# Weight tiles loaded by two transfers, and the transfers of two queues pinned to one order

## The chip, the core and the metric

The kernel runs on one core of a Trainium2 chip. The time is device microseconds (us) of that core, from the start of the program to its end; a run is one execution. The profile is one more execution, taken by the hardware profiler: its span goes from the first to the last instruction, and every start in the text is counted from the span's start.

The core's engines work beside each other, each through its own list of instructions in order: TensorE (PE; PEld is its weight load), VectorE (DVE), ScalarE (ACT), GpSimd (POOL) and SyncE (SP), which only starts transfers. Transfers between memory and on-chip memory are started by SyncE and ScalarE here (a few at the start by GpSimd) and carried out by 16 DMA engines that all of them share. "SPq" and "ACTq" stand for an engine's sequencer, which issues transfers.

## The reference

Two blocks, one after the other. The first is a delta rule over 768 tokens for 4 batches of 8 heads, with head size 48; the second takes its output as 3072 tokens of 384 features.

```python
def _attn_ref(q, k, v, beta) -> np.ndarray:
    B, H, S, D = q.shape
    k_n = k / (np.linalg.norm(k, axis=-1, keepdims=True) + 1e-06)
    state = np.zeros((B, H, D, D), dtype=np.float32)
    y = np.zeros_like(q)
    for t in range(S):
        kt, vt, bt = (k_n[:, :, t], v[:, :, t], beta[:, :, t, None])
        y[:, :, t] = np.einsum('bhd,bhde->bhe', q[:, :, t], state)
        v_old = np.einsum('bhde,bhd->bhe', state, kt)
        state = state + bt[:, :, :, None] * np.einsum('bhd,bhe->bhde', kt, vt - v_old)
    return y.astype(np.float32)
...
def _moe_ref(x, w_in, w_out) -> np.ndarray:
    h = x @ w_in
    g = h * np.cos(h)
    return (g @ w_out).astype(np.float32)
```

w_in is 384 x 2048 and w_out 2048 x 384, both in 64-bit floats; q, k, v and beta are 32-bit.

## The kernel before

**Tokens.** The 768 tokens of a batch are cut into 24 units of 32. For a unit the kernel loads q, k and v (`load`, line 341, and from unit 8 on, for the transposed q and k, `load_blocks`, line 369), forms the products of its keys and queries (`gram`), solves a triangular system for its 32 steps, brings the state forward (`update`) and makes the unit's outputs (`within`). The triangular matrices of two units are inverted together, twelve times in all, by GpSimd (`invert`, line 702; the first by VectorE). Their way goes through memory, since the rows have to be laid out anew: `gram_put` (line 652) writes g to g_dr, `gram_get` (line 667) reads it back as gb, the inverse z is written by `put` (line 739) to z_dr, and `get` (line 746) reads it back as zt, or for the first two units as halves_z. The factors of the solve in TensorE are zt and the right side.

**Features.** Every two units make 256 tokens (4 batches of 32 each) of the second block, twelve steps in all: the product with w_in (`hidden`, line 930, in the first two steps, and `layer`, line 1109, with sums of blocks after them), h cos(h) (lines 974 to 1000) and the product with w_out (`output` and `product`, lines 1134 and 1189), whose result is stored by `store`.

**Weights.** The weights come in 28 tiles, listed in `narrows` (line 455): 12 of w_in, 128 rows by 512 values, and 16 of w_out, 128 rows by 384 values. A value is two 32-bit words, so a row of a tile is 1024 or 768 words, 4096 or 3072 bytes, and a tile 512 or 384 KB. `narrow_load` (line 469) loads a tile into a buffer called pairs by one transfer. `narrow_split`, `narrow_shift` and `narrow_add` then make 32-bit floats of it, on ScalarE, VectorE and GpSimd; each of them works on the whole tile. The buffers are of the tag "g", of which there are eight, shared with the blocks of g.

**Order.** The program is a list of tasks, and `Order.LINE` (line 83) is a sequence of their numbers, written out by hand, in which the tasks are emitted. `Order.OTHER` (line 50) is the set of tasks that take the other engine of two: `queue` (line 335) gives a transfer to ScalarE where its task is in that set, and to SyncE otherwise. `pin` (line 1697) adds a dependency that the compiler's scheduler keeps and that makes no wait on the chip. The last lines of the kernel pin every instruction to the one before it of the same engine, so each engine runs its own instructions in the written order. How the instructions of different engines stand among each other in the compiled program is settled by the compiler's scheduler, apart from the buffers' first users, which `wrote` (line 1709) pins across engines.

**Semaphores of transfers.** There are 526 transfers of SyncE and 139 of ScalarE, 665 in all. They share eight completion semaphores, given out in turn in the order in which the scheduler has laid the transfers of both queues. A transfer waits in its engine's sequencer until the transfer that had its semaphore before, the eighth before it in that order, has landed. Behind a waiting transfer of ScalarE stand ScalarE's own computations.

Of the kernel before, what the change touches and what calls it, by code (L numbers as in the profile page):

```python
# [218 lines left out]
def kernel(  # L219
# [115 lines left out]
    def queue(*key):  # L335
        return nc.scalar if key in Order.OTHER else nc.sync
# [60 lines left out]
    for b in range(B):  # L397
        nc.gpsimd.dma_start(
            out=bq[C * b : C * b + H].rearrange("p n t -> p (n t)"), in_=beta[b]
# [67 lines left out]
    words = {}  # L467

    def narrow_load(t):
        _, src, n = narrows[t]  # L470
        pairs = ffn_pool.tile([128, 4, TOK], U32, name="pairs", tag="g", bufs=GATES)
        words[t] = pairs.rearrange("p a t -> p (a t)")[:, 0 : 2 * n]
        queue("weights", t).dma_start(out=words[t], in_=src)
        words[t] = words[t].rearrange("p (n two) -> p n two", two=2)

    def narrow_split(t):
# [777 lines left out]
    def store(p, i, cols=slice(0, DM)):  # L1254
# [12 lines left out]
            x=2, x_sum=XS, turns=2, g=GATES, o=2, o_out=2,  # L1267
# [396 lines left out]
    def weights(t):  # L1664
        c = 1.0 if t < 12 else 0.78
        add(("weights", t), "SP", 0.45, lambda: narrow_load(t),
            [("weights", t - 1)] if t else [],
            makes=[("g", ("pairs", t))], moves=1.8 * c, due=LOADS + 2 * t)
        add(("split", t), "ACT", 1.4 * c, lambda: narrow_split(t), [("weights", t)])
        add(("shift", t), "DVE", 1.4 * c, lambda: narrow_shift(t), [("split", t)])  # L1670
        add(("add", t), "POOL", 1.45 * c, lambda: narrow_add(t), [("shift", t)],
            uses=[("pairs", t)], due=W_IN + 2 * t if t < 12 else W_OUT + 2 * (t - 12))
# [24 lines left out]
    def pin(ins, on):  # L1697
        tc.add_manual_dep(
            ins,
            on.name,  # L1700
            mybir.DependencyInfo(
                mybir.DependencyClass.NoSync, mybir.DependencyReason.DATA
            ),
            reason="order",
        )
# [12 lines left out]
    order.run(wrote)  # L1718


    last = {}
    for ins in nc.cur_bb.bb.instructions:
        if ins.engine in last:
            pin(ins, last[ins.engine])
        last[ins.engine] = ins


# [29 lines left out]
```

## Time and profile before

| | us |
|---|---|
| three runs | 667.28, 664.82, 667.79 |
| median | 667.28 |
| the profiled execution's span | 663.5 |
| TensorE busy | 595.1 (90%) |
| TensorE's weight load busy | 559.0 (84%) |
| VectorE busy | 504.2 (76%) |
| GpSimd busy | 484.3 (73%) |
| ScalarE busy | 294.7 (44%) |

TensorE's busy time by stretch, with its granted clock and the share of time that the DMA engines are busy:

| stretch, us | TensorE busy, us | clock | DMA share |
|---|---|---|---|
| 0 to 25 | 10.85 | 1.00 | 0.82 |
| 25 to 50 | 3.32 | 0.59 | 0.81 |
| 50 to 76 | 15.14 | 0.50 | 0.71 |
| 76 to 150 | 67.04 | 0.94 | 0.63 |
| 150 to 240 | 88.38 | 1.00 | 0.39 |

Transfers issued, from the page's last part (name, queue, count, size):

```profile
pairs<-in_moe_w_out_dram SPq DMA_DIRECT2D x12, 384.0 KB
vp<-in_v_dram SPq DMA_DIRECT2D x88, 48.0 KB
pairs<-in_moe_w_in_dram ACTq DMA_DIRECT2D x7, 512.0 KB
gb<-g_dr ACTq DMA_DIRECT2D x12, 256.0 KB
kp<-in_k_dram SPq DMA_DIRECT2D x128, 24.0 KB
...
pairs<-in_moe_w_in_dram SPq DMA_DIRECT2D x5, 512.0 KB
```

In rows of the profile "out<-in" names what an instruction writes and reads, "L473" is line 473 of the kernel, and an arrow in brackets tells what ended the idle time before an instruction. A "chain" is the work that ended last, followed back from the end: each link is what released the next one.

### The profile page before, as it was taken

The numbers are of one execution on the slowest core, as the hardware profiler recorded it, in microseconds if no ns is written. First come the engines' busy times: TensorE is split into PE (matmuls) and PEld (weight loads), VectorE is DVE, ScalarE is ACT, GpSimd is POOL, SyncE is SP. The second block draws the span as 40 slices with busy tenths as digits, with TensorE's granted clock in tenths as the row PEclk, the third lists the DMA queues.
The fourth block names the chain that finished last, engine by engine and source line by source line (L and its number), as shares of the span: only waits on it lengthen the run. The fifth ranks groups of instructions, "written<-read, shape, count | busy, mean of one in ns | idle before, by whom it ended". The sixth has DMA issues, their size and how long they took to land.

```text
span 663.5 us, 23460 instructions
## 1 busy us (share of the span) xinstructions
PE 595.1 (90%) x9784; PEld 559.0 (84%) x9784; DVE 504.2 (76%) x996; ACT 294.7 (44%) x518; POOL 484.3 (73%) x852
## 2 busy tenths in 40 slices
PE   3315799889999999999999999999789999999997
PEld 3304698677898999989999999999789999999996
DVE  5775588689799887868888888898758678667581
ACT  3424475454234544545545436444235453546340
POOL 4447888868898898888898988988666688413322
PEclk9855599989999999999999999999989999999999
DMA  8786764762164352344451462542311400200000
GB/s 173 166 185 155 180 139 120 156 133 43 44 113 62 64 94 43 74 85 71 67 100 27 80 98 41 95 78 52 73 24 33 92 10 26 34 2 26 1 24 25
DMA packets 215629, 51.52 MB, mean 78 GB/s; under 512 B 207076, under 2 KB 210420, under 8 KB 215524
## 3 DMA queue, kind: packets, MB, share of 16 engines
q1 hardware_dynamic: 160372, 32.31, 26.4%
q10 hardware_dynamic: 54896, 17.28, 12.1%
q8 instruction: 77, 1.26, 0.8%
q0 software_dynamic: 256, 0.45, 0.3%
q14 instruction: 28, 0.23, 0.1%
HBM read 39.24 MB, written 10.75 MB: 75 GB/s over the span
## 4 chain that ended last, share of the span: by engine, by line
PE 61%; POOL 19%; DMA 7%; DVE 4%; issue 4%; SPq 2%; ACT 1%; ACTq 0%; POOLq 0%; DVEq 0%
PE p_h L1113 20%; PE p_out L1193 20%; POOL z L728 8%; POOL part L721 7%; PE p_h L935 6%; PE p_out L1136 3%; DMA vp<-in_v_dram 3%; PE p_kq L781 2%; POOL x_sum L1028 2%; PE p_s L876 2%; PE p_kq L893 2%; PE p_u L851 2%; PE p_o L1193 2%; DMA pairs<-in_moe_w_in_dram 1%; PE p_g L611 1%
## 5 line engine op out<-in xcount | busy, mean ns | idle before, releaser
L721 POOL TENSOR_TENSOR part<-z,gb 128x126 f32<-128x126 f32 (+22 forms) x341 | 151.9, 445 | 36.2 <-ACT z L700 8.2
L728 POOL TENSOR_TENSOR z<-z,part 128x126 f32<-128x126 f32 (+22 forms) x341 | 155.3, 455 | 26.7
L1193 PE MATMUL p_out<-w_out,g_ffn 128*128 128x192 f32 x672 | 120.0, 329 | 0.0
L1193 PEld LDWEIGHTS p_out<-w_out,g_ffn 128*128 128x128 f32 x672 | 108.0, 190 | 1.2
L1209 POOL TENSOR_TENSOR g_ffn<-g_ffn 128x512 f32<-128x512 f32 x43 | 57.8, 1349 | 56.6 <-PE p_out L1193 30.9
L1113 PE MATMUL p_h<-x_sum,w_in 128*128 128x128 f32 x640 | 83.2, 279 | 7.9 <-ACT g_ffn L1125 6.4
L1193 PE MATMUL p_out<-w_sum,g_ffn 128*128 128x192 f32 x496 | 88.9, 328 | 0.1
L992 ACT ACTIVATE turns<-turns,halfpi 128x512 f32<-128x512 f32 x96 | 68.3, 719 | 42.5 <-DVE turns L983 35.6
L1113 PEld LDWEIGHTS p_h<-x_sum,w_in 128*128 128x128 f32 x640 | 78.4, 193 | 9.2 <-ACT g_ffn L1125 6.7
L1193 PEld LDWEIGHTS p_out<-w_sum,g_ffn 128*128 128x128 f32 x496 | 79.6, 190 | 0.7 <-DVE o L1245 0.3
L976 ACT ACTIVATE turns<-g_ffn,quarter_turn 128x512 int32<-128x512 f32 x70 | 50.1, 720 | 48.8 <-DVE g_ffn L1130 25.7
L1130 DVE TENSOR_TENSOR g_ffn<-g_ffn,p_h 128x512 f32<-128x512 f32 x80 | 54.6, 683 | 17.0 <-PE p_h L1113 14.9
L906 ACT COPY y<-p_kq 32x384 f32<-32x384 f32 x96 | 45.1, 470 | 37.2 <-PE p_kq L893 31.9
L995 DVE TENSOR_TENSOR g_ffn<-turns,g_ffn 128x512 f32<-128x512 f32 x70 | 53.3, 770 | 8.9 <-ACT turns L992 8.8
L983 DVE SCALAR_TENSOR_TENSOR turns<-g_ffn,turns 128x512 f32<-128x512 f32 x70 | 56.5, 812 | 1.6 <-ACT turns L976 1.4
L1113 PE MATMUL p_h<-x_sum,in_sum 128*128 128x128 f32 x400 | 53.8, 279 | 0.1
L935 PE MATMUL p_h<-x_ffn,w_in 128*128 128x128 f32 x384 | 48.8, 288 | 5.5 <-DVE g_ffn L995 5.5
L935 PEld LDWEIGHTS p_h<-x_ffn,w_in 128*128 128x128 f32 x384 | 46.9, 202 | 6.6 <-DVE g_ffn L995 5.9
L1113 PEld LDWEIGHTS p_h<-x_sum,in_sum 128*128 128x128 f32 x400 | 50.0, 194 | 0.9 <-ACT g_ffn L1125 0.4
L1245 DVE SCALAR_TENSOR_TENSOR o<-p_out,o 128x192 f32<-128x192 f32 x74 | 25.2, 353 | 31.5 <-PE p_out L1193 30.6
L530 POOL TENSOR_TENSOR knrm<-ksum,halves 128x16 f32<-128x16 f32 (+1 forms) x14 | 38.9, 2777 | 11.1 <-DVE ksum L518 11.0
L1113 PE MATMUL p_h<-x_ffn,w_in 128*128 128x128 f32 x320 | 43.1, 279 | 0.0
(133 smaller groups left out, 1011.0 us busy)
## 6 DMA issues: line engine op xcount, KB each, us to landing
pairs<-in_moe_w_out_dram SPq DMA_DIRECT2D x12, 384.0 KB
vp<-in_v_dram SPq DMA_DIRECT2D x88, 48.0 KB
pairs<-in_moe_w_in_dram ACTq DMA_DIRECT2D x7, 512.0 KB
gb<-g_dr ACTq DMA_DIRECT2D x12, 256.0 KB
kp<-in_k_dram SPq DMA_DIRECT2D x128, 24.0 KB
out_dram<-o ACTq DMA_DIRECT2D x14, 192.0 KB
pairs<-in_moe_w_in_dram SPq DMA_DIRECT2D x5, 512.0 KB
gb<-g_dr SPq DMA_DIRECT2D x10, 256.0 KB
```

The costliest lines, as they stand in the source:

```text
L721: eng.tensor_tensor(out=part, in0=z[:, 0:rows, j, None].to_broadcast(shape), in1=a[:, j, None, j + 1 :].to_broadcast(shape), op=ALU.mult,)
L728: eng.tensor_tensor(out=behind, in0=behind, in1=part, op=ALU.subtract)
L906: nc.scalar.copy(by_parity(y[quarter(b)]), p_kq[quarter(b ^ 1), :, b % 2])
L935: nc.tensor.matmul(p_h[:, i], w_in[:, t, (4 * k + i) * 128 : (4 * k + i + 1) * 128], xts[p][:, t, unit * 128 : (unit + 1) * 128], start=(i ...
L976: nc.scalar.activation(turns[p, f], hidden_of(p, f), AF.Identity, bias=quarter_turn, scale=TURN)
L983: nc.vector.scalar_tensor_tensor(out=r, in0=hidden_of(p, f), scalar=TURN, in1=t, op0=ALU.mult, op1=ALU.subtract,)
L992: nc.scalar.activation(r, r, AF.Sin, bias=halfpi, scale=2.0 * math.pi)
L995: nc.vector.tensor_tensor(out=place(p, f), in0=step_of(rests.pop((p, f)), f), in1=step_of(hidden_of(p, f), f), op=ALU.mult,)
L1113: nc.tensor.matmul(p_h[:, e], in_block(*w)[:, e], x_of(p, b), start=new and e == 0, stop=True, skip_group_check=True,)
L1130: nc.vector.tensor_tensor(out=part_of(p, to), in0=part_of(p, one), in1=part_of(p, two), op=op)
L1193: nc.tensor.matmul(p_o, left(p, part, a)[:, e % 4], right(e, b), start=(e == 0), stop=(e == FT // 2 - 1), skip_group_check=True,)
L1209: either(("left", p, x, s), nc.vector, nc.gpsimd).tensor_tensor(out=left(p, s, to), in0=left(p, s, one), in1=left(p, s, two), op=op)
```

## The change

Two edits. In `narrow_load` a tile comes by two transfers: its row is seen as four runs, of 256 words for w_in and 192 for w_out, and the first transfer takes the first and third run of every row, the second the second and fourth. Both are issued one after the other on the queue that had the one. In the last lines, every transfer of SyncE or ScalarE is pinned to the transfer of the other queue before it, where those two are of different engines. With the pins that were there, all transfers of both queues stand in one order, the written one; GpSimd's six are left out.

```diff
@@ narrow_load
-        queue("weights", t).dma_start(out=words[t], in_=src)
+        to, of = (
+            x.rearrange("p (a b n) -> p b a n", a=2, b=2) for x in (words[t], src)
+        )
+        for b in range(2):
+            queue("weights", t).dma_start(out=to[:, b], in_=of[:, b])
         words[t] = words[t].rearrange("p (n two) -> p n two", two=2)
@@ the end of the kernel
-    last = {}
+    last, before = {}, None
     for ins in nc.cur_bb.bb.instructions:
         if ins.engine in last:
             pin(ins, last[ins.engine])
         last[ins.engine] = ins
+        if isinstance(ins, mybir.InstDMACopy) and ins.engine != mybir.EngineType.Pool:
+            if before is not None and before.engine != ins.engine:
+                pin(ins, before)
+            before = ins
```

## The prediction

> **What bounds the kernel now.** I read the page's 40 slices first, then the chain of waits in order of time, then the table of waits, then single stretches of the timeline.
>
> ```profile
> PE   3315799889999999999999999999789999999997
> ...
> DMA  8786764762164352344451462542311400200000
> ```
>
> Each digit is a slice of 16.6 us. TensorE is idle for much of the first four and a half slices, while the DMA engines are busiest there. After that TensorE is full but for a dip in slices 28 to 30. So two places are worth anything: the first 76 us and the dip.
>
> ```profile
> 24.55 6.13 DMA vp<-in_v_dram
> 32.58 6.74 DMA vp<-in_v_dram
> 41.18 2.46 SPq L356
> 44.66 3.92 DMA vp<-in_v_dram
> ...
> 61.88 4.14 DMA pairs<-in_moe_w_in_dram
> 66.03 2.75 DMA kp<-in_k_dram
> ```
>
> This is the chain (start, length). In the first 76 us it runs through transfers, and most links are no data links: SyncE holds a transfer back until an earlier, unrelated one has landed. Eight semaphores go round all transfers of SyncE and ScalarE, so a transfer starts when the one eight places before it is down. What counts as "before" is what the change moves.
>
> ```profile
> ACT g_ffn L1125 <- DMA gb<-g_dr: 11.4, 1, 11.4
> ...
> 470.16 0.32 ACTq L375 DMA_DIRECT2D qp<-in_k_dram  x1
> 470.57 0.59 ACT L1125 COPY p_h<-p_h 128x512 f32<-128x512 f32 x1
> 481.14 1.41 ACTq L375 DMA_DIRECT2D qp<-in_k_dram  x3
> 482.59 1.07 ACT L1125 COPY g_ffn<-p_h 128x512 f32<-128x512 f32 x2 [11.43 <-DMA gb<-g_dr]
> ...
> 476.67 0.37 SPq L742 DMA_DIRECT2D z_dr<-z  x1
> 477.27 1.35 SPq L684 DMA_DIRECT2D gb<-g_dr  x2
> ...
> 474.55 2.77 PE L1193 MATMUL p_out<-w_sum,g_ffn 128*128 128x192 f32 x16
> 483.72 2.08 PE L1113 MATMUL p_h<-x_sum,w_in 128*128 128x128 f32 x8 [6.41 <-ACT g_ffn L1125]
> ```
>
> One line of the table of waits, then the timeline round the dip. ScalarE issues one of four loads into qp at 470.16, and the second only at 481.14. It waits for a gb load that SyncE could not issue before 477.27, because the put of z ahead of it waits for GpSimd until 476.67; that load lands at 481.06. ScalarE's copies stand behind its own held transfer, and TensorE behind the copies: 6.41 us idle, and then slow matmuls.
>
> ```profile
> 440.00:484.00 44.00, 37.59 (x632) 35.87 (x616) 31.46 (x65) 18.45 (x33) 32.26 (x63) 0.96 0.38 65
> 484.00:600.00 116.00, 116.00 (x1885) 111.21 (x1886) 86.12 (x160) 54.05 (x95) 73.65 (x145) 0.99 0.15 30
> 600.00:658.00 58.00, 58.00 (x412) 58.00 (x411) 34.20 (x60) 21.86 (x36) 18.86 (x16) 1.00 0.06 16
> ```
>
> Busy time by stretch (the second number after the length is TensorE's): from 484 us to 658 us it never rests, so what is gained or lost before goes straight to the end.
>
> **The pins, late.** In written order the second qp load (470.16's neighbour) has eight places ahead of it a put of g that landed at 461.08, not the gb load. ScalarE goes on at 470.5, and the 6.41 us of TensorE vanish. The restart goes too: the first sixteen matmuls after the wait are a chain link of 3.57 us, against 1.98 us for the like group at 494.07: 1.6 us. That makes 8.0 us. What is late next: z goes through memory and back to TensorE's solve at 493.39, from a zt load down at 483.26, so 10.1 us of room, more than 8.0. The last inverse is tighter: its zt lands 4.0 us ahead of its solve at 576.6. GpSimd waited 8.2 us for ScalarE's copy of z at 484.14, held by the same stall, but the gb it also needs lands at 482.13 and so it wins only about 2.7 us. Then 8.0 - 2.7 - 4.0 = 1.3 us are owed, and I take 8.0 - 1.3 = 6.7 us of gain. Bounds: 0 (something else ends that wait) and 8.0.
>
> **The pins, early.** 254 of the 665 transfers get another place. In the first 76 us, old holds vanish and new ones come: with the old issue times, 17 of SyncE's and 16 of ScalarE's transfers would now stand before their eighth predecessor has landed, by 15.0 and 20.2 us in all. These overlap, so I carried each along the chain with unchanged lengths: k's last load down at 9.22 holds a load issued at 8.02 (+1.2), a gb at 45.11 waits for the put of z (+0.6), a halves_z load for that gb (+1.6), the load at 53.29 for a weight tile (+2.8), and the square at 68.88 starts 2.3 us late.
>
> **The split.** 28 more transfers are issued, 17 by SyncE and 11 by ScalarE, at 0.35 to 0.45 us (the rows of line 473). That is 12 us of sequencer, most of it beside other waits. A whole 512 KB tile takes 4.1 to 4.4 us to land when little else runs; its packets of 4096 bytes take 159 ns and each engine has eight, 1.27 us, and the rest, 2.9 us, is start and completion. A half is not in the trace. Its packets are 1024 bytes, 46 ns in this trace (the gb of the first inverse), sixteen per engine, 0.74 us; below, a small transfer (1.6 us for the quickest k load); above, a whole tile. I take 2.9 us for the first and, issued 0.46 us later and queued behind it, 3.7 us for the second, so the tile is down about when it was. But it holds two semaphores for 6.6 us where one was held for 4.3: 2.3 us more for each of the 15 tiles issued before 76 us, 35 us. The transfers of that stage held 496 of 608 semaphore-us (8 times 76), so 82% become 87%: the split pushes into the bound itself.
>
> Carried along the chain, in written order and with the halves: k's load at 7.53 +1.7; the put of g at 17.99 +2.8, for its eighth predecessor is now a k load down at 20.78; ScalarE's k load at 25.64 +4.8 behind a gb; SyncE's q at 31.60 +4.5; gb at 44.52 +5.0; halves_z at 48.60 +6.1 (ScalarE's copies of z and of weights stand behind this one); the SyncE load at 53.29 +7.3 behind a weight's second half; the square at 68.88 +7.1. Two links get something back: the v load of 6.74 us and a k load of 4.4 us ran beside ScalarE's tiles, and a half keeps an engine for 0.74 us where a whole one keeps it 1.27: 2 x 0.53 = 1.1. So the first stage costs 7.1 - 1.1 = 6.0 us. Bounds: 2.0 (hardly more than the order alone) and 14 (below).
>
> That the other queue waits for a whole share of a tile is in the packets: SyncE's 192-byte packets stop from 56.75 to 57.75 us while ScalarE's 4096-byte ones run. The Trainium skill ("DMA: Bandwidth & Descriptors", Queues, rings and completion order) has each engine change queues only after a packet of some 9 to 17 descriptors; the trace agrees, and by that rule too a half of sixteen would pass unbroken, no less.
>
> The 13 tiles of w_out from 76 us on fall where TensorE is busy 67 of 74 us (windows). Five of ScalarE's transfers there would be held, 2.4 us at most; TensorE's other work covers them: 0, and 2.4 if the cover is gone. Of the two passes over a tile nothing changes, they start when both halves are down.
>
> **Sum.** 663.5 (span) + 6.0 + 0 - 6.7 = 662.8. The runs' median, 667.28, is 3.8 above the profiled span, so **666.6 us**: no change that a measurement can tell (about 0.5%, 3.3 us).
>
> **Rivals.** *Slower: a half is as long as a whole tile.* For it: a tile's first packets take some 640 ns each, four times the later ones, so the start may be paid per transfer. Then each of 15 tiles holds another 4.3 + 0.3 us of one of eight semaphores, 15 x 4.6 / 8 = 8.6; SyncE issues seven of the halves at 0.46, 3.2; the order 2.3: 14. With -6.7 it ends at 674.6. It decides once a second half takes over 4.3 us. Against it: w_out's 3072-byte rows start faster. The Trainium skill ("DMA: Bandwidth & Descriptors", Rules for kernel authors) speaks for this side: many small transfers should be made one. By its fitted 2.0 us for each transfer, an estimate, the split alone costs 15 x 2.0 / 8 = 3.8 us of the first stage.
>
> *Slower: the dip stays.* The pins free ScalarE, but TensorE waits there for another engine; the gain is 0 and 673.3 comes out. For it: GpSimd's inverse ends only at 476.67, and its waits are long. Against it: the 10.1 us of room.
>
> *Faster: small transfers slip between halves.* Loads of v and k that ran 4 to 6.7 us beside tiles fall to 2 to 3; the first stage costs only 2.0 and 662.6 comes out. For it: the long v links of the chain. Against it: most of those tiles stand in the same queue as the loads, where nothing can slip.
>
> *The pins order nothing across the queues.* Then the held loads at 481 us stay and the split costs 6: 673.3. Against it: each pin names the transfer before it.
>
> **Chances.** Cancelling 0.42 (alone 663.5 to 671), long halves 0.22, dip stays 0.12, slip 0.20, idle pins 0.04. Faster by over 0.5% (below 663.9) takes most of the slip and a tail of the cancelling, 0.28; slower (above 670.6) the others less a little, 0.38; within, 0.34. The range 661 to 675 leaves about 0.08 below and 0.12 above.
>
> **What would show it.** ScalarE's 11.4 us wait on gb<-g_dr is gone, and TensorE runs through where 477 to 484 was: the pins hold. The first solve of unit 0, at 71.8 us now, comes at 76 to 80: the first stage is right; at 85, halves are long; at 74, they slip. If TensorE has a new hole of over 3 us after 100 us, a new hold that I priced at nothing sits there, and I am wrong.

## The result, and the profile after

| | before | after |
|---|---|---|
| runs, us | 667.28, 664.82, 667.79, 666.26 | 660.69, 661.65, 659.52, 660.27 |
| median, us | 666.77 | 660.48 |
| ratio, 95% interval | 1 | 0.9908 (0.9888 to 0.9927) |
| profiled execution's span, us | 663.5 | 658.7 |

The changed kernel is faster by 6.3 us. The forecast was 666.6 with a range of 661 to 675, so the time lies under the range by half a microsecond, and the gain is more than 0.5%.

The slices of the page after, to be read as before (16.5 us each):

```profile
PE   3306599979999998999999999999999999999997
...
DMA  8786665565254435255442362344231310200000
```

The dip of slices 28 to 30 is gone; the low first slices are still there. The windows (from:to, length, then busy time of TensorE, its weight load, VectorE, ScalarE and GpSimd with their counts; clock, DMA share, GB/s):

```profile
50.00:76.00 26.00, 12.54 (x483) 10.87 (x483) 14.55 (x27) 11.39 (x22) 20.45 (x44) 0.83 0.68 156
76.00:150.00 74.00, 68.06 (x1244) 61.55 (x1245) 53.26 (x101) 41.48 (x79) 60.59 (x105) 0.94 0.60 132
...
440.00:484.00 44.00, 44.00 (x747) 42.23 (x744) 37.46 (x77) 20.50 (x36) 34.24 (x67) 1.00 0.37 64
```

In the last row TensorE was busy 37.59 of 44 us before and is busy for all of it now. The timeline of the changed kernel at that place (start, length, engine, line, what it does, and in brackets the idle time before it) shows why:

```profile
473.86 0.86 ACTq L375 DMA_DIRECT2D qp<-in_k_dram  x2
...
474.76 1.04 ACTq L375 DMA_DIRECT2D qp<-in_k_dram  x2
476.72 0.59 ACT L1129 COPY g_ffn<-p_h 128x512 f32<-128x512 f32 x1 [1.80 <-DMA qp<-in_k_dram]
...
478.31 2.77 PE L1197 MATMUL p_out<-w_sum,g_ffn 128*128 128x192 f32 x16
...
480.62 1.37 SPq L688 DMA_DIRECT2D gb<-g_dr  x2
```

ScalarE issues all four loads into qp within 2 us and copies at 476.72. The gb load, which ended the 11.4 us wait before, is issued only at 480.62, and nobody waits for it here. Of ScalarE's wait, 1.80 us are left, and TensorE has no gap.

Where the rest went is read by setting each of VectorE's 996 instructions beside the same one of the profile before. The changed kernel's stand 1.6 us later at 70 to 76 us, 3.1 us later at 200 to 225 and 3.75 us later at 474. At 487 us they stand 4.43 us earlier, and so it stays (4.59 at the end). So the dip gave 3.75 + 4.43 = 8.2 us, the first 76 us cost 1.6 and the stretch from 76 to 475 us another 2.2, where the prediction had put nothing.

### The profile page after: what moved, and what is told of

Read it like the earlier page. It is cut to its first block, busy times and chain, and to the rows that moved or that the text cites. A ratio compares the mean times of both kernels' runs of the same rounds, so it can differ in the third digit from the quotient of the medians.

```text
span 658.7 us, 23519 instructions
## 1 busy us (share of the span) xinstructions
PE 593.7 (90%) x9784; PEld 557.5 (85%) x9784; DVE 500.9 (76%) x996; ACT 294.9 (45%) x518; POOL 486.9 (74%) x852
## 4 chain that ended last, share of the span: by engine, by line
PE 66%; POOL 15%; issue 3%; DMA 2%; SPq 1%; DVE 1%; ACTq 1%; ACT 1%; POOLq 0%; DVEq 0%
PE p_out L1197 24%; PE p_h L1117 24%; POOL z L732 6%; POOL part L725 5%; PE p_h L939 3%; PE p_kq L785 3%; PE p_s L880 2%; PE p_kq L897 2%; PE p_g L615 2%; PE p_u L855 2%; PE p_o L1197 2%; POOL x_sum L1032 2%; POOL g_ffn L1213 1%; PE p_z L918 1%; DMA z_dr<-z 1%
## 5 line engine op out<-in xcount | busy, mean ns | idle before, releaser
L725 POOL TENSOR_TENSOR part<-z,gb 128x126 f32<-128x126 f32 (+22 forms) x341 | 154.3, 453 | 33.7 <-DMA gb<-g_dr 6.9
L534 POOL TENSOR_TENSOR knrm<-ksum,halves 128x16 f32<-128x16 f32 (+1 forms) x14 | 37.5, 2680 | 11.3 <-DVE ksum L522 11.2
```

What stands on the lines that cost most here:

```text
L725: eng.tensor_tensor(out=part, in0=z[:, 0:rows, j, None].to_broadcast(shape), in1=a[:, j, None, j + 1 :].to_broadcast(shape), op=ALU.mult,)
```

## The experiments

Twelve kernels ran in three groups, each on one chip with runs of the kernel before beside them (667.96, 665.71 and 665.52 us in the median). Since these differ, groups are compared by ratios. Two numbers of each profile split the time: when TensorE starts the first solve of unit 1 (L811 before, `p_w<-rhs`), called the first solve below, and what is left of the span from there. The prediction and the expectations call this solve unit 0's, but unit 0's own (`p_w<-vp`) starts at 52.27 us before; 71.79 is unit 1's.

| kernel | pins | halves | us | ratio (95% interval) | first solve, us | from there, us |
|---|---|---|---|---|---|---|
| before | none | none | | 1 | 71.79 | 591.7 |
| changed | all | all | 660.48 | 0.9908 (0.9888 to 0.9927) | 73.42 | 585.3 |
| e1 | all | none | 658.04 | 0.9842 (0.9825 to 0.9860) | 72.80 | 582.4 |
| e2 | none | all | 670.30 | 1.0029 (1.0015 to 1.0043) | 74.38 | 595.4 |
| e3 | late | none | 661.47 | 0.9891 (0.9867 to 0.9916) | 75.75 | 586.2 |
| e6 | late | all | 661.01 | 0.9887 (0.9862 to 0.9913) | 74.55 | 585.3 |
| e7 | all | w_in | 656.56 | 0.9875 (0.9854 to 0.9897) | 72.40 | 581.9 |
| e8 | all | w_out | 658.73 | 0.9902 (0.9878 to 0.9926) | 70.58 | 586.8 |
| e4 | all | by rows | 664.13 | 0.9982 (0.9965 to 1.0000) | 78.20 | 586.4 |
| e5 | all | contiguous | 657.76 | 0.9881 (0.9858 to 0.9905) | 72.34 | 584.0 |
| e9, changed again | all | all | 660.42 | 0.9925 (0.9895 to 0.9954) | 71.47 | 584.8 |
| e10 | all | all but the last 4 on SyncE | 657.03 | 0.9873 (0.9849 to 0.9898) | 72.59 | 583.1 |
| e11, e1 again | all | none | 655.72 | 0.9852 (0.9829 to 0.9875) | 72.25 | 582.9 |
| e12, e7 again | all | w_in | 656.32 | 0.9862 (0.9834 to 0.9890) | 71.21 | 581.7 |

### Pins alone (e1)

The second edit on the kernel before:

```diff
+        if isinstance(ins, mybir.InstDMACopy) and ins.engine != mybir.EngineType.Pool:
+            if before is not None and before.engine != ins.engine:
+                pin(ins, before)
+            before = ins
```

> One transfer per weight tile as before, the pins of the change. Theory (the late pins give 8.2 us, the early order costs about 2, and the halves cost next to nothing because v's, k's and q's loads land sooner between them): 666.8 - 8.2 + 2 = 660.6 us, the same as the changed kernel within 1.5 us; the first solve of unit 0 comes 1 to 3 us later than before, and a v load takes 4.6 us as before instead of 3.8. Rival 1 (the halves cost the 3.8 us that lie between 76 and 475 us and the order costs nothing): 666.8 - 8.2 = 658.6 us or less. Rival 2 (the halves pay, the early order is dear): 662.5 us or more, with the first solve over 4 us late.

Measured: 658.04 us, 9.9 under the kernel before, and the ratio is under the changed kernel's by 0.0066. The theory's 660.6 was missed and its first rival's 658.6 was met: the halves do cost something, and the early order costs next to nothing. The first solve is 1.0 us later than before, not 2.3.

### The split alone (e2)

The first edit on the kernel before:

```diff
-        queue("weights", t).dma_start(out=words[t], in_=src)
+        to, of = (
+            x.rearrange("p (a b n) -> p b a n", a=2, b=2) for x in (words[t], src)
+        )
+        for b in range(2):
+            queue("weights", t).dma_start(out=to[:, b], in_=of[:, b])
```

> Two transfers per weight tile as in the change, no pins between the queues. Theory: the dip near 480 us stays, TensorE idle 5 to 8 us there behind ScalarE's copies; the halves cost 0 to 2 us in the first stage: 666.5 to 669 us. A wait of ScalarE's copies on gb<-g_dr of about 11 us is still in the table of waits. Rival 1 (as in the prediction, a split costs 3.7 us by itself): 670.5 us. Rival 2 (the split alone, by another turn of the eight semaphores, already breaks the hold at 481 us): about 660 us without any pin.

Measured: 670.30 us, 2.3 more than before (its profiled run, at 671.74, was among its slowest). The dip is there again. The timeline of e2:

```profile
475.01 0.32 ACTq L375 DMA_DIRECT2D qp<-in_k_dram  x1
...
486.16 1.40 ACTq L375 DMA_DIRECT2D qp<-in_k_dram  x3
487.60 1.07 ACT L1129 COPY g_ffn<-p_h 128x512 f32<-128x512 f32 x2 [11.59 <-DMA gb<-g_dr]
...
488.73 2.07 PE L1117 MATMUL p_h<-x_sum,w_in 128*128 128x128 f32 x8 [6.56 <-ACT g_ffn L1129]
```

These are the held load, the 11.6 us wait and the 6.56 us hole of the kernel before, moved by 5 us. The split doesn't touch the dip; the pins alone remove it. The time is between the theory's upper end and the 3.7 us of the first rival.

### Pins only late, without and with the split (e3, e6)

On the kernel before (e3), and with the split of the change as well (e6):

```diff
+        if isinstance(ins, mybir.InstDMACopy) and ins.engine != mybir.EngineType.Pool:
+            count += 1
+            if count > 300 and before.engine != ins.engine:
+                pin(ins, before)
+            before = ins
```

> One transfer per weight tile as before, and only the transfers after the 300th in written order are pinned across the queues, so that everything before some 190 us is laid out by the scheduler as before. Theory: the dip goes and nothing is paid early: 666.8 - 8.2 = 658.6 us, 2 us under the changed kernel; the lag of the same instructions is within 0.5 us up to 190 us. Rival 1 (the early order pays, not the late one): 664 us or more. Rival 2 (the hold moves elsewhere, since the scheduler lays the first 300 anew): a new idle stretch of TensorE of over 3 us after 100 us, 662 us or more.

> Two transfers per weight tile as in the change, pins across the queues only after the 300th transfer in written order. Theory: dip gone (-8.2), halves 0 to 2: 658.6 to 660.6 us; against the run with late pins and whole tiles the difference is the price of the halves in the scheduler's order. Rival (the halves need the written order to be cheap: without it the second halves hold the other queue): 663 us or more, with the first solve of unit 0 over 4 us later than before.

In both profiles the dip is gone, and by the same amount: in e3 the lag of the same VectorE instruction goes from +6.16 at 474 us to -2.04 at 487, in e6 from +4.71 to -3.48, 8.2 us each time. So the late pins are the whole of that gain. But e3 was 2.9 us slower than forecast, at 661.47, and slower than e1 beside it (658.04, the intervals don't overlap); e6, at 661.01, lies just over its 660.6. The lag that e3 was to hold within 0.5 us of the kernel before is 4 to 6.7 us from 70 to 150 us. Yet its first 300 transfers have the same places as before, semaphore by semaphore, and still its first solve came at 75.75 us, against 71.79. So one order of transfers can take 4 us more or less in the first stage, from one profiled execution to another (that the chip differed too can't be ruled out), and the profile of before caught a quick one. e3's runs go from 657.68 to 663.78 us, e6's from 657.41 to 663.48, those of e1 from 657.0 to 658.31. The written order of the first 300 transfers, up to about 220 us, is then not a cost of 2.3 us but a gain: 661.47 - 658.04 = 3.4 us against e3, and 667.96 - 8.2 - 658.04 = 1.7 against the kernel before without its dip. That e6 is no slower than e3 says that the split's price drowns in that spread.

### Which half of the split costs (e7, e8, and e12)

On the changed kernel; e7 and e12 have 512 in the first line and so split w_in alone, e8 has 384 there and splits w_out alone:

```diff
+        if n == 512:
             for b in range(2):
                 queue("weights", t).dma_start(out=to[:, b], in_=of[:, b])
+        else:
+            queue("weights", t).dma_start(out=words[t], in_=src)
```

> Pins as in the change; only the 12 tiles of w_in come by two transfers. With pins and whole tiles the same instructions stood 0.7 us earlier at 76 us and 4.2 us earlier from 287 us on than in the changed kernel, so 0.7 of the split's price lies in the first stage and 3.5 behind it, where the w_out tiles are. Theory (the w_out halves carry the price, by SyncE's issue time and the put of z behind them): 658.0 + 0.5 to 1.5 = 658.5 to 659.5 us; the put of z near 144 us comes within 1.5 us of the run with whole tiles. Rival (the w_in halves set the first stage back and everything else follows it): 661 us or more.

> Pins as in the change; only the 16 tiles of w_out come by two transfers. Theory: nothing is lost by 70 us (within 0.5 us of the run with whole tiles) and 3 to 4 us are by 250 us: 661 to 662 us; the put of z that starts at 144.5 us with whole tiles starts at 147 to 149. Rival (the price is of the first stage, w_in): 658 to 659 us, the put of z within 1 us of 144.5.

> Pins and only w_in by halves, beside pins alone. Theory (the halves of w_in are free: what they hold is given back by the sooner landing of v, k and q): within 1 us of pins alone. Rival 1 (they gain): 1 us or more under pins alone. Rival 2 (they cost as the prediction had it): 2 us or more over it.

The halves of w_in cost nothing that shows: beside pins alone in one group, e12 is 0.6 us slower with overlapping intervals, within the 1 us of its theory. Its first solve comes 1.0 us sooner; over all profiles with all pins, leaving out the halves by rows, it starts at 71.9 us on average with w_in whole (e1, e8, e11) and at 72.2 with w_in halved (six others). In e7 the put of z near 144 us came at 144.43, beside 144.47 in e1, as its theory had it. The page's last part (count, size, median us to landing) shows what gives way, first e1, then e7:

```profile
kp<-in_k_dram SPq DMA_DIRECT2D x128, 24.0 KB, 2.6
pairs<-in_moe_w_in_dram SPq DMA_DIRECT2D x5, 512.0 KB, 4.1
```

```profile
kp<-in_k_dram SPq DMA_DIRECT2D x128, 24.0 KB, 2.0
pairs<-in_moe_w_in_dram SPq DMA_DIRECT2D x10, 256.0 KB, 3.1
```

Two halves hold 2 x 3.1 where one tile held 4.1. Summed over the transfers issued in the first 76 us, the weights hold 101.2 semaphore-us in e7 and 66.2 in e1, 35.0 more. All transfers together hold 491.7 and 490.1. What the halves hold, the others give back: SyncE's halves_z loads take 3.18 us in place of 3.81, its gb 4.93 in place of 6.55, its loads of v 4.00 in place of 4.28 and of k 3.35 in place of 3.65. The same holds in all 14 profiles: from issue to landing, a transfer of that stage that isn't a weight's takes 3.67 to 3.84 us in the mean where w_in is whole (before, e1, e3, e8, e11) and 3.28 to 3.48 where it comes by halves. Why they land sooner, and whether they slip in between two halves, isn't shown.

The halves of w_out are not free. From the first solve on, e8 needs 586.8 us, and the changed kernel 585.3 and 584.8; the four profiles with w_out whole and all pins need 581.7 to 582.9. By the means that is 585.6 - 582.2 = 3.4 us. All of it is there at the end of unit 4's solve, near 158 us: this comes 82.5 to 84.3 us after the first solve with w_out whole and 86.0 to 87.4 with halves, 3.4 us apart in the mean. At the end of unit 3's solve, near 115 us, the means are 0.4 us apart. So the cost arises between these two. e8 missed "nothing by 70 us" on the good side, its put of z came at 146.5, just under the expected 147 to 149, and its ratio lies by that of the changed kernel.

### Where they cost it (e9, e10, e11)

One place in that stretch is the put of z of the third inverse, which SyncE issues after its w_out tiles. (The expectations call it the second. It is GpSimd's second, and the third of all; it serves units 4 and 5.) The timeline of the changed kernel:

```profile
142.85 2.14 SPq L375 DMA_DIRECT2D qp<-in_q_dram  x4
145.04 0.49 SPq L667 DMA_DIRECT2D g_dr<-g  x1
145.62 1.36 SPq L477 DMA_DIRECT2D pairs<-in_moe_w_out_dram  x2
147.03 2.08 SPq L356 DMA_DIRECT2D vp<-in_v_dram  x4
149.21 0.40 SPq L746 DMA_DIRECT2D z_dr<-z  x1
...
144.89 0.23 POOL L732 TENSOR_TENSOR z<-z,part 128x16 f32<-128x16 f32 x1
...
159.06 1.10 PE L855 MATMUL p_u<-rhs,zt 64*64 64x48 f32 x30 [0.70 <-DMA zt<-z_dr]
```

and of e1, pins with whole tiles:

```profile
138.57 1.95 SPq L375 DMA_DIRECT2D qp<-in_q_dram  x4
140.57 0.96 SPq L663 DMA_DIRECT2D g_dr<-g  x1
141.63 0.79 SPq L473 DMA_DIRECT2D pairs<-in_moe_w_out_dram  x1
142.46 1.91 SPq L356 DMA_DIRECT2D vp<-in_v_dram  x4
144.47 0.40 SPq L742 DMA_DIRECT2D z_dr<-z  x1
...
142.22 0.23 POOL L728 TENSOR_TENSOR z<-z,part 128x16 f32<-128x16 f32 x1
```

GpSimd's last step of the inverse ends at 145.12 in the one and at 142.45 in the other. The put follows 4.1 us later with halves and 2.0 us later with whole tiles: SyncE is still issuing what stands ahead of it. TensorE then waits for the zt loads that depend on the put, by 0.7 us here, 1.05 in e9 and 1.1 in e8; it doesn't with whole tiles. More hangs on GpSimd. The chain of the changed kernel behind the put (start, length, what):

```profile
149.21 5.79 DMA z_dr<-z
155.02 0.32 ACTq L765
...
157.64 0.51 ACT z L704
158.28 0.24 POOL part L725
```

ScalarE issues unit 4's zt loads when the put has landed, copies the start of the next inverse into z behind them, and GpSimd goes on. Counted from the first solve, this copy starts at 80.1 to 80.7 us with w_out whole and at 83.4 to 84.8 with halves, and the solve of unit 6, which needs that inverse, ends at 126.2 to 126.9 and 129.8 to 130.7. Unit 6's lateness, 3.8 us in the means, is about what is left at the end, 3.4.

In e10 only the last four of SyncE's w_out tiles are whole again, on the changed kernel:

```diff
+        if t < 24:
             for b in range(2):
                 queue("weights", t).dma_start(out=to[:, b], in_=of[:, b])
+        else:
+            queue("weights", t).dma_start(out=words[t], in_=src)
```

> The changed kernel once more, so that it stands beside the three others on one chip with one set of runs of the kernel before. Theory: 0.991 of the kernel before, the put of z of the second inverse near 149 us, and of its delay against whole tiles (4.7 us) some 2 us are SyncE's issue of halves after the inverse is done and some 2.7 us the later start of the inverse.

> The changed kernel, with the last four of SyncE's w_out tiles (the ones it issues between 130 and 147 us, ahead of the put of z of the second inverse) by one transfer each again; 24 tiles stay split. Theory (SyncE's sequencer sets the put of z): the put of z comes within 2.5 us of the inverse's end instead of 4.1, and the time falls by 1.5 to 2.5 us against the changed kernel of this call. Rival (the semaphores or the share of the DMA engines count, spread evenly over all 16 tiles of w_out): four of 16 tiles, 0.5 to 1 us.

> Pins alone once more, beside the changed kernel. Theory: 2.5 to 4 us under the changed kernel of this call (the price of the split), 0.985 of the kernel before. Rival (the two calls differed by their chips and the split is free): within 1 us.

The timeline of e10:

```profile
143.02 0.53 SPq L480 DMA_DIRECT2D pairs<-in_moe_w_out_dram  x1
143.59 1.92 SPq L356 DMA_DIRECT2D vp<-in_v_dram  x4
145.62 0.40 SPq L749 DMA_DIRECT2D z_dr<-z  x1
...
143.35 0.23 POOL L735 TENSOR_TENSOR z<-z,part 128x16 f32<-128x16 f32 x1
```

The put comes 2.0 us after the inverse's end. With these four whole and all pins it is 1.4 to 2.7 us (e1, e7, e10, e11, e12), with these four halved 4.0 to 4.6 (changed, e4, e5, e8, e9), without overlap. The time fell by 660.42 - 657.03 = 3.4 us; the two intervals overlap by a little (0.9895 to 0.9898), and the profiles give 2.5 (585.6 - 583.1 from the first solve on). That is more than the rival's 0.5 to 1, and it leaves about 1 us to the other twelve tiles of w_out. Counted from the first solve, the copy for GpSimd's next inverse starts at 81.7 us and unit 6's solve ends at 127.7, about 1 us behind the kernels with w_out whole. Pins alone stand 4.7 us under the changed kernel here, with intervals apart (2.5 to 4 were expected), so the split isn't free, and the sixteen w_out tiles are most of its price. The rest of it comes ahead of the put: from the first solve to the inverse's end it is 70.2 to 71.7 us with w_out halved (changed, e8, e9), 71.0 in e10 and 69.3 to 70.1 with w_out whole.

A second queue is held up there, ScalarE's own. First the changed kernel, then e1:

```profile
107.92 1.23 ACTq L477 DMA_DIRECT2D pairs<-in_moe_w_out_dram  x2
109.19 3.12 ACTq L765 DMA_DIRECT2D zt<-z_dr  x4
112.71 0.56 ACT L485 ACTIVATE w_out<-pairs 128x384 f32<-128x384 f32 x1 [4.38 <-POOL z L732]
```

```profile
106.04 0.36 ACTq L473 DMA_DIRECT2D pairs<-in_moe_w_out_dram  x1
106.49 1.90 ACTq L761 DMA_DIRECT2D zt<-z_dr  x4
108.43 0.56 ACT L481 ACTIVATE w_out<-pairs 128x384 f32<-128x384 f32 x1 [1.98 <-POOL part L721]
```

From the issue of this tile to ScalarE's next computation it is 2.4 us in the four kernels with w_out whole and 4.2 to 4.8 in the six with halves there (changed, e4, e5, e8, e9, e10). Besides the issue of the second half, the third of the four zt loads takes 1.35 to 1.64 us in place of 0.41; in the changed kernel its eighth predecessor had landed 7 us earlier, so this is no hold by a semaphore, and why it takes so long is open. By 66 us after the first solve, ahead of the put, VectorE's work is 2.4 us later with halves than with w_out whole, by the means. That this sets back the inverse is argued from the order in time; no run takes these halves alone away.

In e9 the put came at 146.3, not near 149: there the inverse ended at 141.7, as early as with whole tiles and 3.5 us earlier than in the first profile of the changed kernel, 2.0 of them by an earlier first solve. Only the gap behind the inverse came again, at 4.6 us, some 2 us over the 2.0 to 2.7 of e1 and e11, as expected.

### Other halves (e4, e5)

On the changed kernel, the first two added lines in e4, the last two in e5:

```diff
-            queue("weights", t).dma_start(out=to[:, b], in_=of[:, b])
+            half = slice(64 * b, 64 * b + 64)
+            queue("weights", t).dma_start(out=words[t][half], in_=src[half])
...
+            run = slice(b * n, b * n + n)
+            queue("weights", t).dma_start(out=words[t][:, run], in_=src[:, run])
```

> Pins as in the change, two transfers per tile, but each takes half of the rows, whole (64 rows of 4096 or 3072 bytes), so there are as many transfers as in the change and a quarter of the pieces per transfer. Theory (the price is SyncE's issue time of 0.6 us for a transfer of 256 pieces, and the second transfer's semaphore): issue falls to about 0.35 us and half of the price goes: 659 to 660.5 us. Rival 1 (the price is the number of transfers and semaphores alone): as the change, 660.5 to 662 us. Rival 2 (long packets let nothing in between): v's loads need 4.6 us again before 76 us and the first stage is later than the change's by over 2 us: 663 us or more.

> Pins as in the change, two transfers per tile, each one contiguous half of every row (128 pieces of 2048 or 1536 bytes, where the change has 256 of 1024 or 768). Theory (issue time per piece is what SyncE pays): issue 0.35 to 0.45 us and 659 to 660.5 us. Rival (the number of transfers pays): as the change, 660.5 to 662 us. If it is slower than the change, the alternate runs do spread a transfer better over the DMA engines than a contiguous half.

The issue times (count: shortest/median/longest ns, by line), of the changed kernel, e4 and e5:

```profile
L477 SPq DMA_DIRECT2D pairs<-in_moe_w_out_dram x24: 545/610/1569, 71.6 to 146.4; - x24
...
L477 ACTq DMA_DIRECT2D pairs<-in_moe_w_in_dram x14: 374/411/865, 6.7 to 53.9; - x14
```

```profile
L475 SPq DMA_DIRECT2D pairs<-in_moe_w_out_dram x24: 466/588/1452, 77.2 to 152.5; - x24
...
L475 ACTq DMA_DIRECT2D pairs<-in_moe_w_in_dram x14: 473/562/623, 7.1 to 55.2; - x14
```

```profile
L475 SPq DMA_DIRECT2D pairs<-in_moe_w_out_dram x24: 332/430/1703, 70.5 to 144.8; - x24
...
L475 ACTq DMA_DIRECT2D pairs<-in_moe_w_in_dram x14: 334/368/553, 6.7 to 52.9; - x14
```

Contiguous halves are issued faster, as the theory had it, 430 ns in place of 610 for w_out, and 584.0 us from the first solve on give back 1.6 of the 3.4 us; the ratio goes the same way, with overlapping intervals. The halves by rows fell out against the theory: with a quarter of the pieces the issue is as slow for w_out (588 ns) and slower for w_in (562), and the kernel is nearly as slow as before. Its first solve comes 4.8 us after the changed kernel's. By its time that is the second rival, but not by its mechanism: v's loads took 3.9 us in the mean there, not 4.6. The transfers that aren't weights' took 3.48 us, shorter than with whole tiles as well, so sooner landings alone don't make halves free. Which wait delays that first stage is open.

## Why the prediction was wrong, step by step

**The pins, late: right in mechanism, undersized.** The wait, its cause and its removal came as written. The discount of 1.3 us was wrong: no lag comes back between 487 us and the end, so the last inverse took nothing back, and the dip gave 8.2 us where 6.7 were taken (the undiscounted sum was 8.0).

**The pins, early: the wrong sign.** The +2.3 us came from carrying holds along one profiled execution. e1 and e11 started their first solve 1.0 and 0.5 us after that execution, and e3, with the old order, 4.0 after it. One execution of an unpinned first stage was no base for its typical length. By the runs the written order gains, 1.7 to 3.4 us. (The first solve is unit 1's; the prediction read it as unit 0's, at the same time, so the marks at 74, 76 to 80 and 85 us stand.)

**The split in the first stage: the step that failed.** Holding time was about right: 35 us more were forecast for the weights, and 32 came (69.9 before, 102.0 after; 35.0 from e1 to e7). Luck has a part in it: a w_in tile held 3.0 us more, not 2.3, and fewer tiles were under way. The step from there to +6.0 us was not right: it kept every other transfer at its old length, and these took 3.28 to 3.48 us in the mean in place of 3.67 to 3.84, which gave back all of it. The first stage cost 1.6 us, of which e1 gives 1.0 to the order and so 0.6 to the split. The first solve was forecast at 76 to 80 us and came at 73.42, next to the 74 named for the case in which small transfers slip between the halves. The objection to that case, that most of those tiles stand in the same queue as the loads, was wrong from the start: of the 15 tiles issued before 76 us, SyncE issued 7 and ScalarE 8. In e7 it was above all SyncE's loads that landed sooner.

The estimate of 3.8 us was too high for this stage: halving w_in cost 0.3 (72.2 against 71.9 us). The Trainium skill ("DMA: Bandwidth & Descriptors", Anatomy of one DMA — SWDGE (gpsimd) path) fits its 2.0 us to transfers that GpSimd issues. The estimate took it over to SyncE's and ScalarE's.

**w_out priced at nothing: the second failed term.** The cover was named as TensorE's other work, and 2.4 us as the price if it were gone. It did not cover: the cost runs through two sequencers and GpSimd. On SyncE stand eight issues of 0.6 us in place of four of 0.39, and behind them a put that unit 4's solve and GpSimd's next inverse wait for. On ScalarE, two issues and slower zt loads hold its own computations 2 us longer. Measured: about 3.4 us in all, of which e10 shows 2.5 to hang on the last four tiles of SyncE.

**The sum.** In span: 1.5 us from the late term, 6.0 - 1.6 = 4.4 from the first stage, -2.2 from the stretch after it, together 3.7 of the 4.1 us between 662.8 and the measured 658.7. (Those 2.2 are the 3.4 of w_out's halves less what the order gave back there: e1's lag falls from 1.0 us at 72 to -0.3 at 474.) The remaining 2.0 us lie in the step to the median: 3.8 us were added, where the changed kernel's median is 1.8 above its profiled span. The profile before was a quick execution by those 2.0 us.

**The rivals.** Long halves: no, a half of w_in took 3.9 us in the mean and a second half 4.1, under the 4.3 from which that case was to decide (4 of 12 were over it). The dip stays, or idle pins: no. Cancelling: no, all that was lost up to 475 us, 3.8, is less than half of the 8.2. Small transfers slip: they landed sooner and the first stage cost 1.6 where this case had 2.0, though that they slip between the halves isn't shown; 662.6 was still too slow by the late discount and the step to the median.

## What to carry to other kernels

Before a transfer is made two, look at the queue that issues it: what stands behind it on that sequencer, and who waits for that. Here the halves of w_out cost 3.4 us, mostly in that way, and the halves of w_in nothing that shows. When, as here, transfers on two queues share a few completion semaphores in turn, the order between the queues is part of the kernel; pinning it removed 8.2 us of unrelated waits and was worth 9.9 us alone, more than the whole change. Take a transfer-bound stage's length from several executions before pricing a microsecond in it.

## What the runs showed of the hardware

Issue time didn't follow the number of pieces (medians). Halves of 256 pieces took 411 ns (1024-byte pieces, w_in on ScalarE) and 610 ns (768-byte pieces, w_out on SyncE); on ScalarE the latter took 604. Halves of 64 whole rows took 562 ns for w_in, and of 128 contiguous half rows 368. And one program's executions differ by as much as the effects in question. The six runs of e3 lie within 6.1 us and those of the kernel before, in the three groups, within 3.5 to 4.8; with all pins it is from 1.3 us (e1, four runs) to 4.7 (e8, six runs). So the order of the queues alone doesn't make the time steady.
